# Zero fills of two cache gradients as 16 KB rows, and two more of them ahead of a product stage

## The chip, the cores and the metric

The kernel runs on one core of a Trainium2 chip. A core has TensorE (PE in the profile, with PEld for its weight loads), VectorE (DVE), ScalarE (ACT), GpSimd (POOL) and SyncE (SP), and 16 DMA engines that move data between the device memory and the on-chip memory of 128 partitions. The metric is device time in microseconds (us), lower is better. MB in sizes of tiles is 1,048,576 B.

## The reference, cut to what matters

The reference is one decode step of a transformer block (one token, D = 1024) with its backward pass: the output x2 and the gradients of ten inputs. In short:

```
mod  = silu(c) @ w_mod                       # six sections: sa, ca, ga, sb, cb, gb
h1   = layernorm(x) * (1 + ca) + sa
attn = softmax(q k^T / sqrt(128)) v @ wo     # q = h1 @ wq, 32 heads, 4 cache heads, last 4096 of 65536 positions
x1   = x + ga * attn
h2   = layernorm(x1) * (1 + cb) + sb
x2   = x1 + gb * ((sigmoid(h2 @ w_gate) * (h2 @ w_up)) @ w_down)
outputs: x2, and d(x2 . grad_out) / d(x, k_cache, v_cache, wq, wo, w_gate, w_up, w_down, c, w_mod)
```

Attention reads only the last W = 4096 positions of each cache, so the gradients of k_cache and v_cache (out_2 and out_3, each 4 x 65536 x 128 in bf16) are zero at the first 61,440 positions of each of four heads. These are 8 regions of 15 MB, 120 MB in all, and they have to be written. They are about half of the 246.6 MB that the kernel moves.

## The kernel before, in words

The order of every engine's instructions is written out by hand (`manual_schedule`). Most of the on-chip memory is one tile, `arena`, of 192 KB per partition, whose parts are given out by offset (`ar`); small vectors come from `vt` (L104), each a tile of its own.

The stages, with their place in the profile:

- to about 66 us: small loads, the k cache, wq and v loads (1 MB each, rows of 8 KB per partition), the projections and the softmax;
- 66 to about 160 us, the **N stage** (the long product stage): 128 steps of DVE products and PE matmuls (L632, L637);
- about 160 to 315 us, the **B stage**: chunks of a 4096 x 1024 x 1024 product (`bch`, L682 to L701, matmul at L692), and between them the loads and products for ga, cb, sb and gb, sections of w_mod (`b_sec`, `wm_sec` at L338; `mod_tiles` at L344), transposes and folds (`fold_half`, L871);
- about 315 to 464 us, the **feed-forward stage**: seven blocks. A block loads up and gate weights on POOL's queue (`load_ug`, L865), down weights on SP's queue (`load_wd`, L852), reduces them on DVE (`wd_ttr`, L210), overwrites each tile with its gradient and stores it (`store_ug` on POOL, L869; `store_wd` on SP, L855);
- after it, the attention's backward pass and the remaining stores.

The **zero fills** run through all of it. `zeros` (L111) is a tile of 2,048 one-byte zeros per partition. A fill (L169) is one DMA that POOL issues: 128 partitions of 2,048 bytes, cast from one byte to four, become 128 rows of 8,192 B in the region, 1 MB. Each region is cut into 15 such columns of its 120 KB rows, 120 fills in all. Six of them are narrow (L160 to L167, at the places of NARROW, L38): they leave out eight rows, which one early DMA writes (`zero_rest`, L357), and send a small DMA of their own to move on which DMA engine serves a transfer. That leaves 114 full fills.

`zero(n, after)` (L153) issues the next n fills; with `after` the first instruction of each waits for that instruction ("pace"). The tables say how many go where: Z_Q after the q products, Z_SM (4) after the softmax sums (L523), Z_N (31 over the 128 steps) behind the N stage's matmul six before (L640), Z_B behind the B stage's matmul three before (L694), Z_FOLD at its end, Z_FFN in the feed-forward stage, Z_END after it.

POOL issues all fills, most loads and most stores, in program order, on one DMA queue (queue 0). Its completions use eight semaphores in turn, so each transfer that POOL issues waits for the landing of the one eight before it. SP's transfers go to a queue of their own (queue 1); the 16 DMA engines serve both.

Of the kernel before, what the change touches and what calls it, by code (L numbers as in the profile page):

```python
# [10 lines left out]
P = 128  # L11
FP32 = mybir.dt.float32
BF16 = mybir.dt.bfloat16
# [27 lines left out]
def spread(total, n):  # L41
    return [(i + 1) * total // n - i * total // n for i in range(n)]
# [8 lines left out]
Z_KC = [0] * 8  # L51
Z_SM = 4
Z_N = spread(31, 128)
Z_B = [n + (i in (31, 38)) for i, n in enumerate(spread(29, 43))] + [1, 1, 1, 1, 0] + [1, 1, 0, 1, 1, 0, 1, 1] + [1, 0, 1, 0, 1, 0, 0, 0]
# [4 lines left out]
def kernel(  # L59
# [42 lines left out]

    def vt(shape, name, dt=FP32):  # L104
        return pool.tile(shape, dt, name=name)

    ctx.enter_context(tc.manual_schedule())

    ZW = 4096  # L110
    zeros = vt([P, ZW // 2], "zeros", FP8)  # L111
    rows24 = vt([24, P], "rows24", BF16)
    for k, src in enumerate((A_x[0], grad_out[0], c)):
# [5 lines left out]
    make_identity(nc, ident_f)  # L119
    ones_f = vt([P, P], "ones_f")  # L120
    nc.vector.memset(ones_f, 1.0)

    zregions = []
    for og in (out_2, out_3):
        for g in range(G):
            region = og[0, g, 0:SKW, :].rearrange("r d -> (r d)").rearrange("(p x) -> p x", p=P)
            for i in range(region.shape[1] // ZW):
                zregions.append(region[:, i * ZW:(i + 1) * ZW])

    narrow = zregions[0:len(NARROW)]
    wide = zregions[len(NARROW):]
    zleft = []
    while narrow or wide:
        if narrow and (len(zleft) in NARROW or not wide):
            zleft.append((narrow.pop(0), True))
        else:
            zleft.append((wide.pop(0), False))
    nlen = len(NARROW)
    ncount = list(range(1, nlen + 1))  # L140
    NS = SKIP + 1
# [10 lines left out]

    def zero(n, after=None):  # L153
        for _ in range(n):
            if len(zleft) <= keep[0]:
                return
            region, narrow_ = zleft.pop(0)
            first = None
            if narrow_:
                nc.gpsimd.inc_swdge_sem([], [], mode="reset_dge_cursor")  # L160
                n = nlen - ncount.pop()
                first = nc.gpsimd.dma_start(
                    out=rest[0:NS, 0:nlen * 128].rearrange("p (t x) -> p t x", t=2)[:, :, n * 64:(n + 1) * 64],
                    in_=zeros[0:NS, 0:64].rearrange("p (t x) -> p t x", t=1).broadcast_to([NS, 2, 64]))
                ins = nc.gpsimd.dma_start(
                    out=region[8:P, :].bitcast(FP32).rearrange("(t p) x -> p t x", t=2),
                    in_=zeros[0:60, :].rearrange("p (t x) -> p t x", t=1).broadcast_to([60, 2, ZW // 2]))  # L167
            else:
                ins = nc.gpsimd.dma_start(out=region.bitcast(FP32), in_=zeros[:, :])  # L169
            if after is not None:  # L170
                dep(first or ins, after)

# [79 lines left out]
    def total_bcast(part, ncol, name, scale):  # L253
        ps = new_acc("tot_" + name)
        nc.tensor.matmul(ps[:, 0:ncol], lhsT=ones_f[:, :], rhs=part[:, 0:ncol], start=True, stop=True)
        tot = vt([P, ncol], name)
        ts(tot, ps[:, 0:ncol], float(scale), ALU.mult)
        return tot

    def layernorm_col(x_col, name, gap=lambda: None):  # L260
# [7 lines left out]
        sq = vt([P, KD], name + "_sq")  # L268
# [12 lines left out]

    def layernorm_bwd_col(dln, ln, rstd, name):
        part = vt([P, 2], name + "_parts")
        nc.vector.reduce_sum(out=part[:, 0:1], in_=dln, axis=AX.X)
        tmp = vt([P, KD], name + "_tmp")
# [336 lines left out]
    def recent(mm, lag):  # L622
        last_mm.append(mm)
        return last_mm[-lag] if len(last_mm) >= lag else last_mm[0]

    for g in range(G):
        nbank = bank_pair("n_ps", g)
        for t_ in range(KT):
# [7 lines left out]
            for k in range(2):  # L636
                mm = nc.tensor.matmul(nbank[k][:, :], lhsT=k_nat[:, g, t_ * DH:(t_ + 1) * DH],  # L637
                                      rhs=vp[:, t_ % 2, 4 * k:4 * k + 4, :].rearrange("p h d -> p (h d)"),
                                      start=(t_ == 0), stop=False)
            zero(Z_N[s], recent(mm, 6))  # L640
            if t_ == 20:
# [40 lines left out]
    def bch(n=1):  # L682
        for _ in range(n):
# [238 lines left out]
    bch(1)  # L922
    assert not bq
    fold_half(7, 1)
    zero(Z_FOLD[0])
    park(4, ppq, "pq")
# [88 lines left out]
    side(2)  # L1015
    zero(Z_FOLD[2])
    load_wd(1, 0)
    load_wd(1, 1)
    for q in range(NB):
        z = Z_FFN[q]  # L1020
        more = q + 1 < NB
        for j in range(KD):
# [12 lines left out]
            if j == 3:  # L1035
                store_ug(q, 0, 4)
                zero(z[0])
        store_ug(q, 4, 4)
        zero(z[1])
        if more:  # L1040
# [12 lines left out]
            wd_outer(q + 1, 1)  # L1053
            zero(z[2])
            side()
            if q + 2 < NB:
                load_ug(q + 2, 4, 4)
            zero(z[3])
            if q + 2 < NB:
                load_wd(q + 2, 0)  # L1060
                load_wd(q + 2, 1)
        else:
            zero(z[2] + z[3])
    assert not jobs
# [201 lines left out]
    dwq_tile(3)  # L1266
    x2 = vt([P, KD], "x2")
# [4 lines left out]
    dcsum = vt([P, KD], "dcsum")  # L1272
# [3 lines left out]
    t1 = vt([P, KD], "dc_t1")  # L1276
# [4 lines left out]
    dct = vt([P, KD], "dct")  # L1281
    addv(dct, dcs01[:, :, 0], dcsum)
    addv(dct, dct, dcs)
    dcv = vt([P, KD], "dcv")
    mulv(dcv, t1, dct)
# [17 lines left out]
    zero(len(zleft))  # L1303
    assert not zleft and not narrow and not jobs and not bq

# [28 lines left out]
```

## Time and profile before

| what | value |
|---|---|
| time, median of 3 runs (lowest, highest) | 599.83 us (599.76, 601.25) |
| profiled execution: its time, its span | 597.99 us, 596.2 us |
| busy share of the span: PE, PEld, DVE, ACT, POOL | 69%, 47%, 57%, 44%, 27% |
| DMA packets, MB (10^6 B), mean rate | 45026, 246.63, 414 GB/s |
| fills at L169: transfers, size, median us from issue to landing | 114, 1024 KB, 15.3 |
| issue of one fill on POOL, median | 534 ns |

The profile is of one execution. The span runs from the first instruction of the program to the last; the time has some 1.8 us around it. "DMA share" is the time that packets took divided by that of 16 engines; it can pass 1 because the next packet of an engine can begin while one is in progress. A packet is one contiguous row of a transfer, or some short rows together up to 4 KB; for each of its packets the trace records queue, start, duration and size.

### The profile page before, as it was taken

Reading aid. Unit: us, or ns where it says so; the run is one execution under the profiler, and the core shown is the slowest. Engines: PE = TensorE matmul, PEld = TensorE weight load, DVE = VectorE, ACT = ScalarE, POOL = GpSimd, SP = SyncE. Lnnn points to the kernel's source line nnn. Section 1 sums busy time; section 2 is a strip of 40 time slices with the busy share of each in tenths; the row PEclk is TensorE's granted clock in tenths of the full one; section 3 lists DMA queues with packets and bytes.
Section 4 is the critical chain, followed back from the end, with each engine's and each line's share of the span. In section 5 each row is a group of like instructions: output and inputs, shape, how many; then the busy total and the mean of one; then the engine's idle time right before and its main releaser. Section 6 shows DMA issues by size and latency. Waiting matters only on the chain. (4 is left out here: it accounts for less than half of the span.)

```text
span 596.2 us, 11062 instructions
## 1 busy us (share of the span) xinstructions
PE 412.4 (69%) x4612; PEld 278.2 (47%) x4612; DVE 337.7 (57%) x641; ACT 264.6 (44%) x408; POOL 160.6 (27%) x253
## 2 busy tenths in 40 slices
PE   3997688999999989989984444444445184697220
PEld 3996333334344545546654433434334163586220
DVE  3654498999511010070119495797786985698260
ACT  2489514567211014212234572754745733786110
POOL 3113123222223113222221342423423163233100
PEclk9999699999999999999995555555555586755555
DMA  8999999999999999999999999999999999999997
GB/s 349 419 418 421 411 428 411 427 424 425 428 419 423 423 429 423 420 425 423 423 396 411 420 414 408 391 404 415 408 403 416 420 422 414 421 421 423 425 426 319
DMA packets 45026, 246.63 MB, mean 414 GB/s; under 512 B 5085, under 2 KB 5085, under 8 KB 24544
## 3 DMA queue, kind: packets, MB, share of 16 engines
q0 software_dynamic: 37536, 217.60, 95.1%
q1 hardware_dynamic: 7392, 28.32, 12.4%
q8 instruction: 36, 0.59, 0.4%
q14 instruction: 14, 0.11, 0.1%
q10 hardware_dynamic: 48, 0.01, 0.0%
HBM read 60.30 MB, written 185.60 MB: 412 GB/s over the span
## 5 line engine op out<-in xcount | busy, mean ns | idle before, releaser
L692 PE MATMUL b_ps<-arena 128*128 128x512 bf16 x512 | 116.2, 379 | 0.0
L169 POOL DMA_DIRECT2D out_dram<-zeros x114 | 62.8, 553 | 172.0 <-PE n_ps L637 45.5
L837 PE MATMUL tp_side<-ident_bf,arena 128*128 128x128 bf16 x432 | 51.7, 299 | 54.7 <-ACT arena L838 45.9
L193 DVE TENSOR_TENSOR arena<-arena 128x2048 bf16<-128x2048 bf16 x64 | 76.5, 1223 | 2.3 <-PE n_ps L637 0.3
L692 PEld LDWEIGHTS <-arena 128*128 128x128 bf16 x512 | 48.7, 98 | 55.9 <-issue 2.9
L837 PEld LDWEIGHTS <-arena 128*128 128x128 bf16 x432 | 44.2, 140 | 62.3 <-issue 62.0
L838 ACT COPY arena<-tp_side 128x1024 bf16<-128x1024 bf16 x54 | 54.0, 1013 | 41.8 <-PE tp_side L837 40.9
L637 PE MATMUL n_ps<-arena 128*128 128x512 bf16 x256 | 65.8, 378 | 6.2 <-DVE arena L193 4.6
L210 DVE CUSTOM_DVE_ANT_0 arena<-arena,scr 128x1024 bf16<-128x1024 bf16 x56 | 66.2, 1221 | 3.5 <-ACT scr L993 3.5
L210 DVE CUSTOM_DVE_ANT_0 junk<-arena,b1k 128x1024 bf16<-128x1024 bf16 x28 | 34.3, 1224 | 32.6 <-DMA arena<-in_B_w_down_dram 32.0
L637 PEld LDWEIGHTS <-arena 128*128 128x128 bf16 x256 | 24.6, 97 | 41.6 <-issue 16.2
L241 ACT ACTIVATE arena<-scr,h 128x1024 bf16<-128x1024 bf16 x35 | 39.3, 1148 | 0.0
L202 DVE CAST arena<-b_ps 128x512 bf16<-128x512 f32 x6 | 4.2, 692 | 61.6 <-PE b_ps L692 61.6
L1159 PE MATMUL ps_kv<-junk,arena 8*128 8x128 bf16 x256 | 27.1, 304 | 14.1 <-DVE arena L206 12.8
L1163 ACT ACTIVATE arena<-ps_kv 128x512 bf16<-128x512 f32 x48 | 26.2, 686 | 24.2 <-PE ps_kv L1159 23.7
L601 ACT CAST arena<-t_ps 128x512 bf16<-128x512 f32 x56 | 30.1, 589 | 12.1 <-PE t_ps L599 12.1
L869 POOL DMA_DIRECT2D out_dram<-arena x28 | 21.3, 766 | 51.5 <-ACT arena L241 44.8
L1159 PEld LDWEIGHTS <-arena 8*128 8x128 bf16 x256 | 25.2, 140 | 15.9 <-issue 15.8
L993 ACT COPY scr<-tp_dug 128x1024 bf16<-128x1024 bf16 x7 | 7.1, 1012 | 41.4 <-issue 41.4
L456 ACT COPY arena<-tp_wq 128x1024 bf16<-128x1024 bf16 x23 | 21.8, 1034 | 8.1 <-PE tp_wq L454 8.1
L865 POOL DMA_DIRECT2D arena<-in_B_w_up_dram x14 | 10.5, 753 | 48.3 <-DMA out_dram<-arena 26.2
L206 DVE TENSOR_SCALAR arena<-arena,cs_col 128x4096 bf16<-128x4096 bf16 (+1 forms) x16 | 16.0, 1017 | 10.5 <-DMA out_dram<-arena 10.5
(302 smaller groups left out, 646.9 us busy)
## 6 DMA issues: line engine op xcount, KB each, us to landing
out_dram<-zeros POOLq DMA_DIRECT2D x114, 1024.0 KB, 15.3
out_dram<-arena POOLq DMA_DIRECT2D x27, 1024.0 KB, 17.0
out_dram<-arena POOLq DMA_DIRECT2D x30, 512.0 KB, 11.3
out_dram<-arena SPq DMA_DIRECT2D x20, 512.0 KB, 10.7
arena<-in_A_wq_dram POOLq DMA_DIRECT2D x8, 1024.0 KB, 20.7
arena<-in_A_wo_dram POOLq DMA_DIRECT2D x8, 1024.0 KB, 12.0
arena<-in_w_mod_dram POOLq DMA_DIRECT2D x7, 1024.0 KB, 18.1
arena<-in_B_w_down_dram SPq DMA_DIRECT2D x14, 512.0 KB, 10.0
```

Source lines behind the costliest of these rows:

```text
L169: ins = nc.gpsimd.dma_start(out=region.bitcast(FP32), in_=zeros[:, :])
L193: return nc.vector.tensor_tensor(out=out, in0=a, in1=b, op=op)
L210: return nc.vector.tensor_tensor_reduce(out=out, in0=w, in1=b, scale=1.0, scalar=0.0, op0=ALU.mult, op1=ALU.add, accum_out=acc)
L241: return nc.scalar.activation(out=out, in_=b, func=ACT.Copy, scale=col)
L456: nc.scalar.copy(out=blk, in_=tp[:, :])
L601: nc.scalar.copy(out=o, in_=ps)
L637: mm = nc.tensor.matmul(nbank[k][:, :], lhsT=k_nat[:, g, t_ * DH:(t_ + 1) * DH], rhs=vp[:, t_ % 2, 4 * k:4 * k + 4, :].rearrange("p h d -> ...
L692: mm = nc.tensor.matmul(bbank[p][k][:, :], lhsT=a4[:, p, h, :], rhs=wo_t[u][:, a, k * 512:(k + 1) * 512], start=(i == 0 and a == 0), stop= ...
L837: nc.tensor.transpose(tp[:, i * P:(i + 1) * P], blk[:, i * P:(i + 1) * P], ident_bf[:, :])
L838: nc.scalar.copy(out=blk if dst is None else dst, in_=tp[:, :])
L1159: nc.tensor.matmul(ps[:, t4 * DH:(t4 + 1) * DH], lhsT=rows[32 * g:32 * g + HG, t_ * P:(t_ + 1) * P], rhs=hd[32 * g:32 * g + HG, :], start= ...
L1163: nc.scalar.activation(out=o, in_=ps[:, :], func=ACT.Copy, scale=float(scale))
```

## The change

The zero tile gets twice the width, 4,096 bytes per partition. Outside the feed-forward stage two neighbouring fills become one DMA (L180 of the new kernel): 128 rows of 16,384 B, 2 MB. The regions are cut into such pairs, with single columns where a region has an odd number; when single columns run out, a pair is split. In the N and B stages `paced` adds up what the tables owe and issues a pair at the first of its two dates. In the feed-forward stage, at the narrow fills and where one is left over, fills stay single (L185 of the new kernel). Z_SM goes from 4 to 6 and Z_N from 31 to 29, so that the sum is the same. To make room for the wider zero tile, vectors of fewer than 8 words share one tile (`tiny`), the matrix of ones shrinks to a column that is read with a broadcast, rows24 moves into a part of the arena that is free at the start, and some late vectors reuse earlier ones.

```diff
-Z_SM = 4
-Z_N = spread(31, 128)
+Z_SM = 6
+Z_N = spread(29, 128)
...
+    TINY = 124
+    tiny_t = pool.tile([P, TINY], FP32, name="tiny")
+    tiny_n = [0]
+
     def vt(shape, name, dt=FP32):
+        words = shape[1] if dt == FP32 else (shape[1] + 1) // 2
+        if dt in (FP32, BF16) and words < 8:
+            k = tiny_n[0]
+            tiny_n[0] += words
+            assert tiny_n[0] <= TINY
+            t = tiny_t[:, k:k + words]
+            return t if dt == FP32 else t.bitcast(BF16)
         return pool.tile(shape, dt, name=name)
...
-    zeros = vt([P, ZW // 2], "zeros", FP8)
-    rows24 = vt([24, P], "rows24", BF16)
+    zeros = vt([P, ZW], "zeros", FP8)
+    rows24 = ar(144, 0.25)[0:24, :]
...
-    ones_f = vt([P, P], "ones_f")
+    ones_f = vt([P, 1], "ones_f")
...
+    narrow = [zregions[0][:, i * ZW:(i + 1) * ZW] for i in range(nlen)]
+    pairs, singles = [], []
+    for k, region in enumerate(zregions):
+        i = nlen if k == 0 else 0
+        n = region.shape[1] // ZW
+        if (n - i) % 2:
+            singles.append(region[:, i * ZW:(i + 1) * ZW])
+            i += 1
+        pairs.extend(region[:, c * ZW:(c + 2) * ZW] for c in range(i, n, 2))
+    total = 2 * len(pairs) + len(singles) + nlen
+    zleft = [k in NARROW for k in range(total)]
...
-    def zero(n, after=None):
-        for _ in range(n):
-            if len(zleft) <= keep[0]:
-                return
-            region, narrow_ = zleft.pop(0)
+    def zero(n, after=None, paired=True):
+        while n > 0 and len(zleft) > keep[0]:
             first = None
-            if narrow_:
+            n -= 1
+            if zleft.pop(0):
+                region = narrow.pop(0)
...
+            elif paired and n > 0 and pairs and len(zleft) > keep[0] and not zleft[0]:
+                n -= 1
+                zleft.pop(0)
+                ins = nc.gpsimd.dma_start(out=pairs.pop(0).bitcast(FP32), in_=zeros[:, :])
             else:
-                ins = nc.gpsimd.dma_start(out=region.bitcast(FP32), in_=zeros[:, :])
+                if not singles:
+                    pr = pairs.pop()
+                    singles.extend((pr[:, 0:ZW], pr[:, ZW:2 * ZW]))
+                ins = nc.gpsimd.dma_start(out=singles.pop(0).bitcast(FP32), in_=zeros[:, 0:ZW // 2])
             if after is not None:
                 dep(first or ins, after)
+
+    owed = [0]
+
+    def paced(n, after):
+        owed[0] += n
+        if owed[0] > 0:
+            k = owed[0] + owed[0] % 2
+            owed[0] -= k
+            zero(k, after)
...
-            zero(Z_N[s], recent(mm, 6))
+            paced(Z_N[s], recent(mm, 6))
...
-            zero(Z_B[nbq - 1 - len(bq)], recent(mm, 3))
+            paced(Z_B[nbq - 1 - len(bq)], recent(mm, 3))
...
-    zero(Z_FOLD[0])
+    ahead = -owed[0]
+    zero(Z_FOLD[0] - ahead)
...
-                zero(z[0])
+                zero(z[0], None, False)
```

The other calls in the feed-forward stage change in the same way as the last one.

More of the change, by code (lines that the diff above doesn't have):

```diff
@@ L125 @@
         for g in range(G):
[L126 to L138, printed above, removed]
-    nlen = len(NARROW)
+            zregions.append(og[0, g, 0:SKW, :].rearrange("r d -> (r d)").rearrange("(p x) -> p x", p=P))
+    nlen = len(NARROW)
+    narrow = [zregions[0][:, i * ZW:(i + 1) * ZW] for i in range(nlen)]
[9 more added lines that the diff above has]
+    zleft = [k in NARROW for k in range(total)]
     ncount = list(range(1, nlen + 1))
@@ L150, in dep @@
                           reason="pace")
-    def zero(n, after=None):
-        for _ in range(n):
-            if len(zleft) <= keep[0]:
-                return
-            region, narrow_ = zleft.pop(0)
+    def zero(n, after=None, paired=True):
+        while n > 0 and len(zleft) > keep[0]:
             first = None
-            if narrow_:
+            n -= 1
+            if zleft.pop(0):
+                region = narrow.pop(0)
                 nc.gpsimd.inc_swdge_sem([], [], mode="reset_dge_cursor")
-                n = nlen - ncount.pop()
+                k = nlen - ncount.pop()
                 first = nc.gpsimd.dma_start(
-                    out=rest[0:NS, 0:nlen * 128].rearrange("p (t x) -> p t x", t=2)[:, :, n * 64:(n + 1) * 64],
+                    out=rest[0:NS, 0:nlen * 128].rearrange("p (t x) -> p t x", t=2)[:, :, k * 64:(k + 1) * 64],
                     in_=zeros[0:NS, 0:64].rearrange("p (t x) -> p t x", t=1).broadcast_to([NS, 2, 64]))
@@ L166, in zero @@
                     out=region[8:P, :].bitcast(FP32).rearrange("(t p) x -> p t x", t=2),
-                    in_=zeros[0:60, :].rearrange("p (t x) -> p t x", t=1).broadcast_to([60, 2, ZW // 2]))
-            else:
-                ins = nc.gpsimd.dma_start(out=region.bitcast(FP32), in_=zeros[:, :])
+                    in_=zeros[0:60, 0:ZW // 2].rearrange("p (t x) -> p t x", t=1).broadcast_to([60, 2, ZW // 2]))
+            elif paired and n > 0 and pairs and len(zleft) > keep[0] and not zleft[0]:
+                n -= 1
+                zleft.pop(0)
+                ins = nc.gpsimd.dma_start(out=pairs.pop(0).bitcast(FP32), in_=zeros[:, :])
+            else:
+                if not singles:
+                    pr = pairs.pop()
+                    singles.extend((pr[:, 0:ZW], pr[:, ZW:2 * ZW]))
+                ins = nc.gpsimd.dma_start(out=singles.pop(0).bitcast(FP32), in_=zeros[:, 0:ZW // 2])
             if after is not None:
                 dep(first or ins, after)
+    owed = [0]
[5 more added lines that the diff above has]
+            zero(k, after)
     rot = [(psum, "mm")]
@@ L254, in total_bcast @@
         ps = new_acc("tot_" + name)
-        nc.tensor.matmul(ps[:, 0:ncol], lhsT=ones_f[:, :], rhs=part[:, 0:ncol], start=True, stop=True)
+        nc.tensor.matmul(ps[:, 0:ncol], lhsT=ones_f[:, 0:1].broadcast_to([P, P]), rhs=part[:, 0:ncol], start=True, stop=True)
         tot = vt([P, ncol], name)
@@ L258, in total_bcast @@
         return tot
+    bwd_tmp = vt([P, KD], "bwd_tmp")
     def layernorm_col(x_col, name, gap=lambda: None):
@@ L267, in layernorm_col @@
         ts(xc, x_col, mean[:, 0:1], ALU.subtract)
-        sq = vt([P, KD], name + "_sq")
+        sq = bwd_tmp
         part2 = vt([P, 1], name + "_p2")
@@ L284, in layernorm_bwd_col @@
         nc.vector.reduce_sum(out=part[:, 0:1], in_=dln, axis=AX.X)
-        tmp = vt([P, KD], name + "_tmp")
+        tmp = bwd_tmp
         ttr(tmp, dln, ln, part[:, 1:2])
@@ L922 @@
     bch(1)
-    assert not bq
+    assert not bq and owed[0] in (0, -1)
+    ahead = -owed[0]
     fold_half(7, 1)
-    zero(Z_FOLD[0])
+    zero(Z_FOLD[0] - ahead)
     park(4, ppq, "pq")
@@ L1015 @@
     side(2)
-    zero(Z_FOLD[2])
+    zero(Z_FOLD[2], None, False)
     load_wd(1, 0)
@@ L1036 @@
                 store_ug(q, 0, 4)
-                zero(z[0])
+                zero(z[0], None, False)
         store_ug(q, 4, 4)
-        zero(z[1])
+        zero(z[1], None, False)
         if more:
@@ L1053 @@
             wd_outer(q + 1, 1)
-            zero(z[2])
+            zero(z[2], None, False)
             side()
@@ L1057 @@
                 load_ug(q + 2, 4, 4)
-            zero(z[3])
+            zero(z[3], None, False)
             if q + 2 < NB:
@@ L1062 @@
         else:
-            zero(z[2] + z[3])
+            zero(z[2] + z[3], None, False)
     assert not jobs
@@ L1266 @@
     dwq_tile(3)
-    x2 = vt([P, KD], "x2")
+    x2 = a3[:, 0:8]
     mulv(x2, gb, ffn)
@@ L1271 @@
     col_to_row_out(dx0, out_1[0], "dx0", late.pop())
-    dcsum = vt([P, KD], "dcsum")
+    dcsum = a3[:, 8:16]
     addv(dcsum, dcs234[:, :, 0], A3[:, :, 2])
@@ L1275 @@
     stt(dcsum, A3[:, :, 1], rm[:, 1:2], dcsum, ALU.mult, ALU.add)
-    t1 = vt([P, KD], "dc_t1")
+    t1 = a3[:, 16:24]
     ts(t1, sig_c, -1.0, ALU.mult, 1.0, ALU.add)
@@ L1280 @@
     mulv(t1, t1, sig_c)
-    dct = vt([P, KD], "dct")
+    dct = a_lo[:, 0:8]
     addv(dct, dcs01[:, :, 0], dcsum)
     addv(dct, dct, dcs)
-    dcv = vt([P, KD], "dcv")
+    dcv = a_lo[:, 8:16]
     mulv(dcv, t1, dct)
@@ L1303 @@
     zero(len(zleft))
-    assert not zleft and not narrow and not jobs and not bq
+    assert not zleft and not narrow and not pairs and not singles and not jobs and not bq
 _INS = ['A_x', 'A_k_cache', 'A_v_cache', 'A_wq', 'A_wo', 'B_x', 'B_w_gate', 'B_w_up', 'B_w_down', 'c', 'w_mod', 'grad_out']
```

## The prediction, made before the changed kernel ran

> **What bounds the kernel now.** I read the page's slices first, then the queues, the stages in windows, the waits, and last two windows of the DMA view in which only one kind of transfer runs.
>
> ```profile
> DMA  8999999999999999999999999999999999999997
> GB/s 349 419 418 421 411 428 411 427 424 425 428 419 423 423 429 423 420 425 423 423 396 411 420 414 408 391 404 415 408 403 416 420 422 414 421 421 423 425 426 319
> ...
> q0 software_dynamic: 37536, 217.60, 95.1%
> q1 hardware_dynamic: 7392, 28.32, 12.4%
> ```
>
> The 16 DMA engines are busy in every slice but the first and last, at 391 to 429 GB/s. 246.6 MB pass through them, and no compute engine comes near (PE 69%, and 50% of its clock in the later half). Counting the trace's packet records, 16 or more packets are in flight nearly always from 2 us to 588 us. So the time is the sum of what the packets cost, plus about 8 us at the ends. Work taken from the DMA engines shortens the kernel, unless a queue then runs dry; delays elsewhere cost only where one runs dry.
>
> ```profile
> core 0: us, PE busy (x) PEld busy (x) DVE busy (x) ACT busy (x) POOL busy (x), PEclk, DMA share, GB/s
> ...
> 66.00:160.00 94.00, 85.32 (x433) 36.61 (x431) 82.24 (x89) 44.89 (x110) 24.80 (x44) 0.96 1.13 422
> 160.00:300.00 140.00, 134.61 (x1107) 73.57 (x1106) 24.44 (x63) 29.25 (x43) 34.29 (x59) 1.00 1.13 423
> ...
> 315.00:464.00 149.00, 67.67 (x1011) 59.72 (x1009) 112.15 (x234) 81.93 (x93) 48.60 (x70) 0.50 1.08 409
> ```
>
> From 66 to 300 us PE is as full as the DMA engines (85.3 of 94 us, 134.6 of 140). That stage's length belongs to PE. What faster fills save there is not seen there: it leaves a shorter queue for the feed-forward stage, from which on only the DMA engines are full. The third row is that stage, at 409 GB/s.
>
> ```profile
> POOL out_dram L169 <- PE n_ps L637: 45.5, 22, 6.3
> POOL out_dram L169 <- DMA out_dram<-zeros: 36.5, 18, 3.9
> ...
> PE g_ps L344 <- DMA arena<-in_w_mod_dram: 0.7, 1, 0.7
> ```
>
> These are waits from 66 to 315 us. POOL waits 18 times until an earlier fill has landed: it has eight completion semaphores, and its ninth transfer waits for its first. The landings show the queue: a fill issued at 86 us lands after 7.6 us, one at 250 us after 20. PE waits for a load once, for 0.7 us.
>
> **What a row costs.** Two windows of the DMA view, the first with fills alone, the second with loads in 8 KB rows:
>
> ```profile
> DMA packets 709, 5.12 MB, mean 427 GB/s; under 512 B 82, under 2 KB 82, under 8 KB 86
> q0 software_dynamic: 709, 5.12, 114.6%
> ```
> ```profile
> DMA packets 1725, 12.56 MB, mean 419 GB/s; under 512 B 197, under 2 KB 197, under 8 KB 197
> ```
>
> A fill's packets overlap (share 114.6%), a load's do not, and the fill is the faster. In the packet records loads and stores have a median of 309 ns at 8,192 B and 159 ns at 4,096 B: 150 ns for 4,096 B, so 300 ns for the bytes of an 8 KB row and 9 ns that do not grow with them. Between 100 and 300 us one fill lands 2.435 us after the one before it (median). An engine writes 8 rows and one 4-byte completion packet in that time: 2,435 - 8 x 300 = 35 ns per fill do not grow with bytes.
>
> **The change part by part.**
>
> 1. *Pairs.* Of the 114 full fills 80 become 40 pairs in the order of POOL's instructions; 34 single ones, all of the feed-forward stage among them, and the six narrow ones stay. A pair is 8 rows of 16,384 B per engine and one completion: 8 x 600 + 35 = 4.835 us against 2 x 2.435 = 4.870. **Saved: 0.035 us x 40 = 1.4 us.** No queue that carries data has a 16 KB packet in this trace, so I bound it. Upper end, the loads' row: 9 ns for each of 8 rows and a completion of 9 ns are 81 ns a pair, 3.2 us. Lower end: nothing, if the rows are cut in two on their way. A loss per row I exclude: the only 16,384 B packets are the instruction queue's 36, with a median of 1,022 ns, and one such packet at 609 ns (by the slope) beside one fill packet (348 ns) is 957 ns, inside their 10% to 90% span of 936 to 1,090. I take 1.4 us, because fills are what becomes longer.
>
> The Trainium skill's "DMA: Bandwidth & Descriptors", section "Where 436 GB/s comes from", sets a ceiling of 435.2 GB/s for the 16 engines, at which an estimate for 80 MB leaves 2.1 us above the fills' rate and halving it gives 1.05 us; that speaks against the upper end. The same page's "SDMA does more than copy" gives 2,048 elements as the most its inline adder takes at once; the fills cast one byte to four and a 16 KB row has 4,096 elements, so if a cast obeyed that, the saving would be nothing. No run here shows it.
>
> 2. *POOL.* 40 issues of 0.53 us go: 21 us on an engine at 27%. They lie beside the transfers and are worth nothing. The eight semaphores now cover up to 16 MB, so POOL waits less for landings; the order of the bytes in its queue is what counts, and that hardly moves.
>
> 3. *Six ahead, and pairs sent at the first of their two dates.* Fills move ahead of loads in POOL's queue. By count, loads of w_o have 16, 18, 24, 32, 40 fills ahead instead of 14, 15, 23, 31, 39; they are used from 156 us on and land from 69 to 174 us, so this is hidden. The second half of the ga load has 53 ahead instead of 52. It lands at 210.96 us and is used here:
>
> ```profile
> L344 PE MATMUL ga_ps<-cs_bf,arena x64: 162/163/166, 211.9 to 213.5; 128*128 128x1 bf16 x64
> ```
>
> One fill later (+2.4) and 23 pairs cheaper (-0.8) it lands at 212.6: **a new wait of 0.7 us** on PE. Behind it stand the rest of the long products, and behind those the start of the feed-forward stage. It costs nothing while the DMA queue holds 15 to 18 us of work there (a fill issued at 315.8 us lands 17.2 us later); without that cover it costs 0.7. The later loads have as many fills ahead as before, or one more with 6 us to spare (242.95 and 245.48 against 252.0).
>
> 4. *The zero tile's memset* doubles, 0.48 to about 0.97 us, at 0.9 us; DVE's next work comes at 6.18 us. *The ones column, the small tiles in one buffer, the reused tiles at the end:* the same instructions stand in the same order on PE and DVE with the same kinds of waits. ScalarE gains one wait, for loads that ended some 50 us before it. All nothing.
>
> Sum: 597.99 us (the profiled execution; its span is 596.2, and 1.8 lies around it) - 1.4 = 596.6. The median of the three runs is 599.83, 1.84 above the profiled one; I carry the saving to the median: **598.4 us**, 0.23% less. About 0.3%, 1.8 us, is what a measurement of this kernel can tell from no change, so my likeliest case lies within it.
>
> **The rivals.**
>
> *A, the forecast:* 598.4 us, chance 0.42. For it: fills are measured, and the DMA engines are never idle. Its own spread, with runs from 599.76 to 601.25 before, is about 0.8 us either way; 0.12 of the 0.42 falls beyond 1.8 us of gain.
>
> *B, a 16 KB row saves what a load's row shows:* 3.2 us, 596.6, chance 0.28. For it: 9 ns are seen at 2, 4 and 8 KB alike (85, 159, 309). Against it: a fill's packets overlap and already hide half of that.
>
> *C, it does not do what it says:* rows are cut, the packets stay at 8 KB, and only issues go. 599.8 us, chance 0.13.
>
> *D, slower:* a packet holds its engine until it is done, and SP's queue takes turns with POOL's. Beside fills a turn of SP is 159 + 304 = 463 ns; beside pairs 159 + 609 = 768. The w_mod loads on SP at 295.5 and 301.8 us have 8 packets per engine each: 8 x 0.305 = 2.4 us later, and on the second PE already waits. The first down-projection stores (319.29 us) run beside the last fills for 3.5 us: 7.5 turns become 4.5, and 3 packets at 318 ns are made up later, 0.95 us. With the 0.7 us of ga that is 4.1 us, and 599.83 + 4.1 = 603.9, chance 0.17. It decides if the feed-forward stage's chain (store, load, two DVE reductions) and not the queue sets its pace. For it: a fill's time to landing falls from 17 us at 316 to 7 to 9 us at 372, and from 372 to 380 us the rate is 366 and 359 GB/s with fewer than 16 packets in flight for a tenth of the time. Against it: even there the DMA share is 1.01 or more, and the low rate goes with loads in 1 KB rows (382 GB/s from 304 to 312 us, with a full queue).
>
> *How the numbers follow:* faster by over 0.3%: B 0.28 + 0.12 of A = 0.40. Within: 0.30 of A + C 0.13 = 0.43. Slower: D 0.17. The range takes in A, C and B down to 0.6 below its centre, and leaves out D's centre and B's tail: 596.0 to 600.8.
>
> **What would show it.** Pairs: packets of 16,384 B on queue 0, 5,120 of them, and some 427 to 430 GB/s becoming 430 to 434 in windows of fills alone. If the spacing of pairs is 4.87 us or the packets are 8 KB, C holds; at 4.79 us, B. Part 2: waits of POOL for landed fills fall from 36.5 us. Part 3: a wait of PE at the ga product of about 0.7 us. D would show as a longer wait of the g_ps product for w_mod, a feed-forward stage that starts after 315 us, and less than 16 packets in flight more often at 370 to 380 us. The forecast is wrong if the feed-forward stage runs the queue dry, so that what was saved before it is lost as idle engines.

## The result, and the profile after

The changed kernel takes 605.01 us (median of 20 runs, 600.81 to 607.84); the kernel before, on the same chip, 600.02 us (20 runs, 598.32 to 601.95). The ratio is 1.0081, 95% interval 1.0066 to 1.0096: slower by 0.8%, where 598.4 us was forecast. A ratio here and below leaves out single runs over 1.5% above the fastest of their kernel (one each of e4, e9 and e13) and is not the quotient of the medians beside it. The runs of the changed kernel are spread over 7 us, those of the kernel before over 3.6. The profiled execution (607.84 us, span 606.1) is the longest of its 20, so what follows shows the loss at its largest.

From the page of the changed kernel, the slices of the DMA engines and the two queues:

```profile
DMA  8999999999999999999999599999999999999997
GB/s 352 418 418 425 413 429 426 431 428 424 430 426 421 431 429 419 435 419 428 408 412 360 197 404 418 381 397 411 404 405 407 416 420 416 421 419 426 425 423 304
...
q0 software_dynamic: 31776, 217.59, 91.2%
q1 hardware_dynamic: 7392, 28.32, 12.4%
```

The same bytes go out in 5,760 packets less. The loss is seen at once: two slices at 360 and 197 GB/s, where nothing of the kind stood before. The same in windows, now cut at the hole:

```profile
core 0: us, PE busy (x) PEld busy (x) DVE busy (x) ACT busy (x) POOL busy (x), PEclk, DMA share, GB/s
66.00:160.00 94.00, 84.42 (x435) 36.92 (x443) 82.80 (x90) 45.85 (x112) 16.12 (x27) 0.99 1.07 427
160.00:300.00 140.00, 130.75 (x1029) 70.69 (x1045) 24.12 (x62) 26.99 (x40) 23.55 (x39) 0.96 1.07 425
...
328.00:346.00 18.00, 8.10 (x88) 6.91 (x89) 17.01 (x36) 11.41 (x14) 1.94 (x3) 0.50 0.58 206
```

The last of these windows in the kernel before:

```profile
328.00:346.00 18.00, 8.61 (x144) 7.66 (x143) 10.03 (x23) 8.34 (x11) 5.81 (x8) 0.50 1.14 420
```

From 66 to 300 us the queue moves 427 and 425 GB/s instead of 422 and 423: by the packet records 126.33 MB have gone out by 300 us instead of 125.57, a lead of 0.76 MB or 1.8 us. Then 18 us at 206 GB/s; at 380 us the lead has become a lag of 2.94 MB, 7 us. In sum the 16 engines stand idle for 8.5 us between 250 and 480 us, before for 0.3 (from the packets in flight, those of 4 bytes left out; one us means all 16 idle for one us). The second row has one more novelty: PE's clock was 1.00 there before, and is 0.96.

What PE waits for, 66 to 330 us, and the ga product:

```profile
PE g_ps L371 <- DMA arena<-in_w_mod_dram: 6.2, 2, 4.4
...
PE b_ps L719 <- DMA arena<-in_A_wo_dram: 0.9, 1, 0.9
```
```profile
L371 PE MATMUL ga_ps<-tiny,arena x64: 163/163/178, 211.0 to 213.5; 128*128 128x1 bf16 x64
...
  DMA arena<-in_w_mod_dram: 0.8, 1
```

(L371 and L719 are L344 and L692 of the kernel before.) The 0.8 us at ga has the place and the size that were forecast, and the load lands at 212.62 us, forecast 212.6; why the size is luck is said further down. The 0.9 us at 176 us was not: the last load of w_o, with 40 fills ahead of it instead of 39, lands at 175.97. And g_ps, the last product ahead of the feed-forward stage, waits 6.2 us for w_mod instead of 0.7.

The instructions of SP's queue, with the time of the first of each pair, in the kernel before and in the changed one:

```profile
295.49 6.62 SPq L338 DMA_DIRECT2D arena<-in_w_mod_dram  x2
319.29 1.14 SPq L855 DMA_DIRECT2D out_dram<-arena  x2
327.70 4.54 SPq L852 DMA_DIRECT2D arena<-in_B_w_down_dram  x2
```
```profile
301.97 6.62 SPq L365 DMA_DIRECT2D arena<-in_w_mod_dram  x2
332.11 1.62 SPq L882 DMA_DIRECT2D out_dram<-arena  x2
335.43 1.53 SPq L879 DMA_DIRECT2D arena<-in_B_w_down_dram  x2
```

PE's products give the last two w_mod loads free 6.5 us later. The second of them then takes 13.1 us to land (321.41) instead of 7.5 (309.27), the feed-forward stage's first matmul comes at 326.0 instead of 313.2, its first store at 332.1 instead of 319.3, and meanwhile POOL's queue, which has only its own 15 us in hand, runs dry. So three links are to be explained: how waits of 0.8 and 0.9 us become 6.5 us, why 6.5 us become 12.8, and why the queue does not cover that.

In the trace of PE's granted clock there are three stretches of half clock inside the products, 3.4 us each, at 213.9, 224.1 and 258.2 us. The kernel before has none between 73 and 312 us. Each costs up to 1.7 us of PE's time, three 5.1. In this execution PE had come 2.0 us early to the products (b_ps at 154.3 instead of 156.4, the full clock having come sooner); less these, with the two waits, that is 4.8 us, and the md_ps product (sb's) at 288.3 is 4.6 late. A wait of 2.2 us inside its second half, up to 296.6, which the profile puts down to nothing ("issue"), makes it the 6.5. Seven of the traced executions have a wait there (after, e3, e4, e6, e12, e13, e16; 0.5 to 2.4 us), and in each it ends 1.3 to 1.5 us after a 16,384 B packet of the instruction queue q8 has ended (295.10 us here). In the kernel before that packet ends at 282.77, long before PE is there. So PE may be waiting for its own instructions; no run tests it.

### The profile page after: what moved, and what is told of

The parts are those of the page before. It is cut to its first block, busy times and chain, and to the rows that moved or that the text cites. A ratio compares the mean times of both kernels' runs of the same rounds, so it can differ in the third digit from the quotient of the medians.

```text
span 606.1 us, 10967 instructions
## 1 busy us (share of the span) xinstructions
PE 414.2 (68%) x4587; PEld 279.2 (46%) x4612; DVE 338.7 (56%) x641; ACT 264.8 (44%) x408; POOL 138.0 (23%) x213
## 5 line engine op out<-in xcount | busy, mean ns | idle before, releaser
L719 PE MATMUL b_ps<-arena 128*128 128x512 bf16 x494 | 117.8, 389 | 2.1 <-DMA arena<-in_A_wo_dram 0.9
L719 PEld LDWEIGHTS <-arena 128*128 128x128 bf16 x512 | 50.0, 100 | 59.8 <-issue 9.4
L864 PEld LDWEIGHTS <-arena 128*128 128x128 bf16 x432 | 44.8, 142 | 62.3 <-issue 62.1
L180 POOL DMA_DIRECT2D out_dram<-zeros x40 | 21.7, 543 | 134.3 <-PE b_ps L719 52.8
L664 PEld LDWEIGHTS <-arena 128*128 128x128 bf16 x256 | 24.6, 97 | 41.6 <-issue 16.2
L1187 PE MATMUL ps_kv<-junk,arena 8*128 8x128 bf16 x256 | 26.5, 299 | 16.2 <-DVE arena L231 14.3
L185 POOL DMA_DIRECT2D out_dram<-zeros x34 | 19.3, 570 | 32.1 <-PE q_ps L499 14.3
## 6 DMA issues: line engine op xcount, KB each, us to landing
arena<-in_w_mod_dram POOLq DMA_DIRECT2D x7, 1024.0 KB, 16.2
```

The costliest lines, as they stand in the source:

```text
L180: ins = nc.gpsimd.dma_start(out=pairs.pop(0).bitcast(FP32), in_=zeros[:, :])
L864: nc.tensor.transpose(tp[:, i * P:(i + 1) * P], blk[:, i * P:(i + 1) * P], ident_bf[:, :])
L1187: nc.tensor.matmul(ps[:, t4 * DH:(t4 + 1) * DH], lhsT=rows[32 * g:32 * g + HG, t_ * P:(t_ + 1) * P], rhs=hd[32 * g:32 * g + HG, :], start= ...
```

## The experiments

Theory 1, after the traces: the w_mod loads come to stand behind pairs, and that is the loss. Theory 2: the loss begins earlier, with loads that have one fill more ahead of them. Rival: the 16 KB rows themselves, as rival D had it. All ratios are to runs of the kernel before on the same chip (medians 599.35 to 599.60 us).

**One part alone, one part undone**

*e2: six ahead alone, in the kernel before.*

```diff
-Z_SM = 4
-Z_N = spread(31, 128)
+Z_SM = 6
+Z_N = spread(29, 128)
```

> The kernel before with six single fills ahead of the N stage instead of four (29 instead of 31 in it). Theory 1 (the last two w_mod loads on SP's queue stand still behind fills at the end of the B stage): nothing changes there, within 1 us of before. Theory 2 (loads that get one more fill ahead make PE late): the ga loads keep 49 and 52 fills ahead, so within 1 us of before too; w_o loads get 15, 17, 24 ahead and have time. If sending fills ahead were the cause by itself: 3 to 5 us slower than before.

598.88 us, ratio 0.9975 (0.9952 to 0.9998); feed-forward stage at 312.9 us, no half-clock stretch, idle engines 0.6 us. Six ahead is not the loss. It is no proven gain either: e8 below, in effect the kernel before once more, has 0.9982.

*e3: the pairs in rows of 8 KB.*

```diff
-out=pairs.pop(0).bitcast(FP32), in_=zeros[:, :]
+out=pairs.pop(0).bitcast(FP32).rearrange("p (t x) -> p t x", t=2),
+in_=zeros[:, 0:ZW // 2].rearrange("p (t x) -> p t x", t=1).broadcast_to([P, 2, ZW // 2])
```

> The changed kernel with the same 40 pairs at the same places, but each written as two rows of 8 KB per partition. If the 16 KB row is the cause (a packet that holds its engine twice as long): back to within 1 us of before, about 600. Theories 1 and 2 (place and order of the fills, not their rows): still 3 to 6 us slower than before, with a feed-forward stage that starts some 8 to 13 us late. The saving of the rows, if there is any, would show as the difference to the changed kernel: up to 1 us.

607.12 us, ratio 1.0097 (1.0062 to 1.0132), with half-clock stretches at 222.7 and 256.8 us, a wait of 6.9 us at g_ps and 7.2 us of idle engines. The long row is innocent, and with it rival D's mechanism.

*e5: pairs sent at the second of their two dates (and four ahead).*

```diff
-Z_SM = 6
-Z_N = spread(29, 128)
+Z_SM = 4
+Z_N = spread(31, 128)
...
-        if owed[0] > 0:
-            k = owed[0] + owed[0] % 2
+        if owed[0] > 1:
+            k = owed[0] - owed[0] % 2
```

> The changed kernel with four fills ahead again and each pair sent at the second of its two dates, so that no load has more fills ahead of it than before. Theory 2: PE no longer waits for the w_o and ga loads, the SP loads of w_mod are issued at about 295 and 301 us as before, and the time is 598 to 600.5. Theory 1 with another cause of the lateness, or the 16 KB rows as cause: still 3 us or more slower than before.

600.68 us, ratio 1.0014 (0.9990 to 1.0039): w_o's loads have 14, 14, 22, 30, 38 fills ahead and ga's second half 51. No PE wait for either, no half-clock stretch, feed-forward stage at 313.6. Theory 2 holds.

*e4: two pairs taken from between block 0's loads and block 1's and put behind the latter.*

```diff
-... + [1, 0, 1, 0, 1, 0, 0, 0]
-Z_FOLD = (1, 1, 2)
+... + [0, 0, 0, 0, 0, 0, 0, 0]
+Z_FOLD = (0, 5, 2)
```

> The changed kernel with the two pairs that stand ahead of the second block's up and gate loads moved behind these loads. Theory 1: the last two w_mod loads on SP run beside loads in 4 KB packets and land 5 to 8 us after their issue instead of 13 to 15; the feed-forward stage starts by 321 us, the DMA queue is not empty before it, and the time is 598.5 to 601. Theory 2 alone (PE is late by 6 us and everything follows): the w_mod loads may land sooner, but the feed-forward stage still starts 6 us late, 602 to 604.

605.76 us, ratio 1.0077 (1.0041 to 1.0114), expected 598.5 to 601: a miss. The w_mod loads are no longer awaited, and the feed-forward stage begins at 318.1. But the pairs were missing where they had stood: block 1's loads are issued only from 311.2 us on, and from 304 to 320 us the engines move 213 GB/s. And the first store on SP's queue, issued at 324.1 us, now met the moved pairs and took 16.2 us. It cleared the place in question and spoiled two others, so it decides nothing between the theories.

**The first link: one fill**

*e6: the kernel before, one fill earlier.*

```diff
+Z_B[15] += 1
+Z_B[16] -= 1
```

> The kernel before with nothing changed but the date of one 8 KB-row fill: it goes ahead of the second half of the ga load instead of behind it (53 fills ahead instead of 52; every other load keeps its count). It asks what the first link of the chain costs by itself. Theory (a short PE wait is multiplied by the clock): the load lands at 213.4, PE waits 1 to 1.5 us for it, at least one half-clock stretch of 3.4 us follows between 213 and 300 (there is none in the kernel before), so PE is 2.5 to 5 us late at 298, the two w_mod loads on SP's queue go out at 298 or later instead of 295.5, and the time is 601 to 605. Rival, as the prediction had it (a wait costs itself and the full queue hides it): no half-clock stretch, PE 1 to 1.5 us late, time 599 to 600.

607.86 us, ratio 1.0097 (1.0063 to 1.0131). No pairs, no six ahead: one 8 KB-row fill ahead of one load. PE waits 0.8 us at ga, half-clock stretches follow at 214.9, 225.2, 259.3 (6.8 us long) and 300.3, and the feed-forward stage begins at 328.2. Expected were 601 to 605 us: one fill ahead of one load costs more than that, 1.0%, and the whole change 0.8%.

*e13: the reverse, in the changed kernel: one date moved behind the second ga load.*

```diff
+Z_B[14] -= 1
+Z_B[16] += 1
```

> The changed kernel with one date moved behind the second ga load, so that 51 fills stand ahead of it instead of 53; the pairs, the first of the two dates, six ahead and every other load's count stay (the two w_o loads still have 40 instead of 39). It is the smallest undoing. Theory (ga's wait is the first link): the load lands at about 208, PE waits for nothing there, no half-clock stretch from it, feed-forward stage at 313 to 316, time 598.5 to 601. If the late w_o loads (a wait of 0.9 us at 176) suffice to start the same chain: 603 to 607 with half-clock stretches after 176 and no ga wait.

604.28 us, ratio 1.0059 (1.0024 to 1.0094), runs from 600.32 to 609.51. In the profiled execution there is no wait at ga, one of 0.3 us for w_o, and there are stretches at 221.1, 255.2 (6.8) and 296.2. Of the two outcomes written down for it this is the second. So a fill ahead of ga is enough (e6), but ga's wait is not needed. That the 0.3 us brought the stretches is not shown either; the table below says why.

**How a wait becomes three stretches**

The starts of all half-clock stretches of an execution lie a whole number of 3.413 us apart (213.88, 224.12 and 258.25 us in the changed kernel: 3 and 10 times): the clock is judged in windows of a fixed grid. And PE has one long wait of its own in this stage, 2.14 us for the layernorm at about 219 us, in every kernel. Where it lies in that grid sorts the executions (us; "lost" is what PE waited for loads between 100 and 215 us):

| execution | lost | the 2.14 us wait begins, after a window's edge | half clock after it |
|---|---|---|---|
| before, e9 (e8 is a repeat of before) | 0 | 2.67, 2.73 (2.64) | no |
| e11, e14, e15, e2, e5 | 0 | 2.93, 3.05, 3.12, 3.14, 3.15 | no |
| changed, e4 | 1.7, 1.5 | 0.05, 3.41 | yes |
| e3, e10, e12 | 0.5, 0.2, 0.9 | 0.14, 0.17, 0.30 | yes |
| e13, e6 | 0.3, 0.8 | 0.32, 0.62 | yes |
| e16, e17 (below) | 0 | 0.38; 2.86 | yes; no |

Begun at 2.6 to 3.2, the wait lies across an edge and spoils two windows a little; begun at 0 to 0.6 (or just at the edge), it lies in one and takes most of it. Without the time lost it would have begun at 3.0 in e3 and at 2.8 in e12, places that no half clock follows in the other executions. In e13 and e10, whose full clock had come at 67.5 and 67.2 us, it would have begun at 0.0 and 3.3, so there the waits of 0.3 and 0.2 us may not have mattered.

In the changed kernel, e4 and e6 one more stretch comes first, at 213.9, 213.8 and 214.9 us, and there the wait at ga has a part of its own. The window ahead of it holds ga's whole product, of 128x1 matmuls, and the wait; in the changed kernel:

```profile
210.47:213.88 3.41, 2.57 (x69) 2.06 (x68) 0.19 (x2) 0.00 (x0) 0.00 (x0) 1.00 1.06 426
```

In e13 the same product lies in one window without a wait (PE busy for 3.33 us), and no half clock follows at its end. So in the changed kernel both waits and this stretch, 1.7 us more, bring PE to the place in the grid that the table gives.

To see whether the grid is the cause, PE is moved in e16 and e17 without any wait:

*e16 and e17: four, or sixteen, useless matmuls ahead of the ga product in the kernel before.*

```diff
+    idle_ps = new_ps("idle_ps")
+    for i in range(4):        # 16 in e17
+        nc.tensor.matmul(idle_ps[:, :], lhsT=ident_bf[:, :], rhs=v_nat[:, 0, 0:512], ...)
```

> The kernel before with four useless matmuls (128x512, 0.21 us each) put ahead of the ga matmuls: PE comes 0.85 us later to the layernorm at 219 us; no load is late, no fill is moved, and no engine waits more. Grid theory: the 2.1 us wait now begins 0 to 0.3 us into a window of the 3.413 us grid instead of 2.7 us into one and fills it, a half-clock stretch follows at about 223, others near 257, PE is 4 us or more late at 290 and the time is 603 to 608. Rival (a wait for a DMA is what brings the stretches): no stretch, PE 0.85 us late, time within 1 us of the kernel before.

> The same with sixteen such matmuls, 3.41 us, one whole window of the grid. Grid theory: PE comes back to the place in the grid that it has in the kernel before, no half-clock stretch between 200 and 300, PE 3.4 us late at 290, the last w_mod load goes out at 305.2 instead of 301.8, and the time is 599 to 602.5 (the late load may cost something by itself), under that of four matmuls. Rival (more lateness, more loss): over that of four matmuls.

Four take 604.0 us, ratio 1.0066 (1.0044 to 1.0089); sixteen 602.89 us, ratio 1.0053 (1.0033 to 1.0074). The windows of the grid around the layernorm, of the kernel before:

```profile
216.45:219.86 3.41, 2.65 (x14) 1.36 (x12) 0.42 (x3) 0.20 (x1) 0.53 (x1) 1.00 1.16 432
219.86:223.28 3.42, 2.04 (x16) 1.22 (x17) 1.19 (x9) 1.53 (x3) 0.00 (x0) 1.00 1.16 431
```

of e16:

```profile
219.44:222.86 3.42, 1.28 (x15) 0.93 (x14) 1.61 (x11) 0.61 (x2) 0.00 (x0) 1.00 1.15 426
222.86:226.27 3.41, 3.41 (x10) 1.17 (x9) 0.00 (x0) 2.15 (x4) 0.37 (x1) 0.50 1.15 430
```

and of e17:

```profile
219.44:222.86 3.42, 2.86 (x15) 1.45 (x13) 0.31 (x2) 0.14 (x1) 0.53 (x1) 1.00 1.15 426
222.86:226.27 3.41, 1.82 (x15) 1.12 (x16) 1.30 (x9) 1.38 (x4) 0.00 (x0) 1.00 1.17 435
```

The second number is PE's busy time. In e16 it is 1.28 us of one window, and the next runs at 0.50; before it is 2.65 and 2.04, in e17 2.86 and 1.82, and the clock stays at 1.00. Four times the added work, and no stretch between 73 and 300 us in the profiled execution: PE is late by about its 3.4 us (fold product at 269.4 instead of 266.2), where e16 with 0.85 us of work is 5.3 late (271.5). That the place in the grid decides is shown by these traces. The times do not tell the two kernels apart: their intervals overlap, e16's profiled execution (607.23 us) is the longest of its 12, and e17 is over the 599 to 602.5 expected. Its last w_mod load goes out at 305.0 us and makes g_ps wait 4.7 us.

It may also be why the kernel before is steadier: its full clock comes at an edge of the grid, and from there PE runs without a wait for a load, so that ga begins 138.8 to 139.3 us later in all seven executions without a wait that got their full clock at 71.7 to 73.3 us. From its 2.67 to the 3.15 of e5 a margin of 0.5 us is seen to be safe, no more. Its runs of 603 to 606.5 us, which the chips of the experiments have too, were not traced.

**The second link: a load on SP's queue behind fills**

*e8: the two w_mod loads written two chunks later in the kernel before.*

> The kernel before with its two w_mod loads on SP's queue issued one place later each in PE's order, so at about 302 and 308 us, as in the changed kernel, instead of 295.5 and 301.8; no pairs, no other fill moved, no PE wait ahead of them. It asks whether the late loads alone cost the time. Theory (SP's queue stands still while fills are at the front of POOL's): the second load is not down before the fills that follow block 0's loads have gone, so it takes 10 us or more, the feed-forward stage begins at 320 or later instead of 313.2, the DMA engines are idle for 4 us or more between 320 and 350, and the time is 602 to 606. Rival (the queues share; what the changed kernel loses it loses by PE's lateness in the products): the load takes 7 to 8 us as before, the stage begins by 317.5, idle under 2 us, time under 601.

599.12 us, ratio 0.9982 (0.9962 to 1.0002), loads issued at 295.4 and 301.7 as before: SP's queue holds them until the matmuls that read their buffer are done, wherever the line stands. The edit moved nothing, and the run is a second measurement of the kernel before.

*e11: the same with a dependency.*

```diff
+    def late_wm(j):
+        dep(nc.sync.dma_start(out=g_t[j], in_=wm_view[:, j, 5 * D:6 * D]), last_mm[-1])
-    wm_sec(5, 4, 1, 58, nc.sync)
-    wm_sec(5, 5, 1, 60, nc.sync)
+    late_wm(4)      # where (5, 5) stood
+    late_wm(5)      # two chunks later
```

> The kernel before with its two w_mod loads on SP's queue made to wait for later products of PE (an added dependency on the last matmul of the chunk two places on), so that they go out at about 301.8 and 308.1 us as in the changed kernel, with PE itself on time and no half-clock stretch ahead. It asks whether late loads alone cost the time. Theory (a load on SP's queue that is not down when block 0's loads end, at 313, stands behind the fills until about 323): the second load takes 12 us or more, the feed-forward stage begins at 322 or later, the DMA engines are idle for 3 us or more between 320 and 350, and the time is 602 to 606. Rival (the queues share, and the loss belongs to PE's lateness): the load lands within 8 us, the stage begins by 317.5, time under 601.

606.38 us, ratio 1.0121 (1.0091 to 1.0152), with PE on time and no half-clock stretch. The loads go out at 301.0 and 305.8 us, and the second lands at 319.1. PE's waits and the windows of e11:

```profile
PE g_ps L344 <- DMA arena<-in_w_mod_dram: 11.1, 2, 10.2
```
```profile
320.00:350.00 30.00, 15.91 (x252) 14.06 (x250) 21.09 (x44) 16.29 (x20) 6.16 (x9) 0.50 0.91 332
```

So late w_mod loads alone bring the loss. Why the second takes 13 us is seen in the DMA view, 302 to 308 us before:

```profile
q0 software_dynamic: 425, 1.58, 71.1%
q1 hardware_dynamic: 331, 0.67, 31.2%
```

and 309 to 315 us after, with SP's two loads outstanding all the time:

```profile
q0 software_dynamic: 191, 2.55, 105.7%
q1 hardware_dynamic: 34, 0.06, 21.5%
```

Beside block 0's loads, whose rows are 1,024 B (four of them to a 4,096 B packet), SP's queue q1 sends 331 packets in 6 us. Beside pairs it sends 34. In e11, beside fills of 8 KB, 312 to 317 us:

```profile
q0 software_dynamic: 279, 2.01, 106.8%
q1 hardware_dynamic: 68, 0.11, 24.1%
```

By then only 56 rows of SP's two loads were left there, and they took 4.3 us. In the kernel before the fills behind block 0's loads come to the front from 308 us on and are alone on queue 0 from 313; the last w_mod load, landed at 309.27, was just ahead of them, and 6.5 us late it isn't.

*e9 and e12: the other way round, one w_mod load made early.* It goes to b1k (issued at 266.8 us in e9), is copied to its home by ACT, and the last load takes the first one's place.

```diff
...
+    g_t[4] = b1k
+    nc.sync.dma_start(out=b1k, in_=wm_view[:, 4, 5 * D:6 * D])
     load_wd(0, 0)
...
-    wm_sec(5, 4, 1, 58, nc.sync)
+    wm_sec(5, 5, 1, 58, nc.sync)
...
-    wm_sec(5, 5, 1, 60, nc.sync)
...
+    nc.scalar.copy(out=ar(60, 2), in_=b1k)
...
```

> The changed kernel with the first of the two w_mod loads put into a buffer that is free 50 us earlier (it is copied to its home by one ACT copy afterwards), so that only one load is gated by the last products, at the place in PE's order where the first one was (about 301.9 us instead of 308.3 for the last one). Pairs, six ahead, late loads of w_o and ga, half-clock stretches: all unchanged. Theory (the loss falls where w_mod's loads come to stand behind pairs): the last load goes out at the date that it has in the kernel before, lands by 312, the feed-forward stage begins at 318 to 320, idle engines under 3 us, time 600 to 602, 3 us or more under the changed kernel. Rival (6 us of lateness of PE is lost at the end whatever the loads do): 604 to 606, with the idle time at another place.

> The kernel with one fill ahead of the second ga load (607.9) and the early w_mod load added: the half-clock stretches stay, the last w_mod load goes out one place sooner in PE's order. Theory (the loss is the load that comes to stand behind fills, PE's lateness of 5 to 8 us costs little by itself): last w_mod load issued at about 306 instead of 312.4, feed-forward stage at 318 to 322 instead of 328.2, idle engines under 3 us instead of 7.7, time 600 to 603. Rival (lateness is lost whatever the loads do): 606 to 609.

e12 (e6 with the early load): 600.36 us, ratio 1.0025 (1.0001 to 1.0048), where e6 has 607.86. Three of e6's four half-clock stretches are there (223.8, 257.9 for 6.8 us, 298.9; none at 214), PE is 6.2 us late at the fold product (e6: 7.8), and the last load, issued at 304.3, lands at 313.2; feed-forward stage at 321.4, idle engines 3.0 us. By the medians PE's lateness by itself costs about 1 us and the load behind fills the other 7. But the profiled execution of e12, in which the lateness is seen, took 602.85 us, and that of e6 609.20: between these two the split is nearer 3 and 6.

e9 (the changed kernel with it): 601.15 us, ratio 0.9994 (0.9964 to 1.0025), runs from 597.86 to 606.87. Its profiled execution had no stretch at all, so it tells nothing of that link; what its six runs over 602 us lose is not known. It tells something of the first. The last w_o load and the second ga load land at 176.03 and 212.67 us, as in the changed kernel, and PE waits for neither, because its full clock came at 73.3 us and not at 67.1, and it is 2.3 us later at b_ps. So whether the same fills make PE wait depends on the execution. The runs of the changed kernel lie in two groups (nine at 600.8 to 603.6 us, nine at 606.6 to 607.8), which would fit; only one of them was traced.

**Versions that might beat both**

> The kernel before with six fills ahead instead of four and the same early w_mod load (no pairs): a version that may beat both. Theory: the last w_mod load goes out at 294.7 instead of 301.0, the feed-forward stage begins 2 to 4 us before 312.9, and the time is 597 to 599 (0.2 to 0.5% under the kernel before); were the stage's start not what sets the end, 598.9 as with six ahead alone.

> Pairs sent at the second of their dates, four ahead (600.7), with the early w_mod load: a version that may beat both kernels and shows what the pairs are worth when no load is late. Theory: feed-forward stage begins at 308 to 312, no idle engines, time 597 to 599, which is the 1.4 us of the pairs and up to 1 us more under the kernel before. If the pairs save nothing: 599 to 600, as the kernel before.

> The changed kernel (pairs, six ahead) with pairs sent at the second of their dates, so that no load has more fills ahead of it than in the kernel before plus one, and the early w_mod load: all three parts of what was learned. If pairs save what the fills' landings say (0.03 to 0.035 us for each of 39 pairs): no half-clock stretch, 597 to 598.5, 0.8 to 1.5 us under the same without pairs (598.9). If their saving is used up elsewhere: 598.5 to 600.

| kernel | us | ratio to before | range of runs |
|---|---|---|---|
| e2: six ahead | 598.88 | 0.9975 (0.9952 to 0.9998) | 598.0 to 602.2 |
| e10: six ahead, early load | 598.90 | 0.9974 (0.9956 to 0.9991) | 598.0 to 599.7 |
| e15: pairs at the second date, six ahead, early load | 599.13 | 0.9981 (0.9957 to 1.0005) | 598.1 to 600.8 |
| e14: the same, four ahead | 600.95 | 1.0021 (1.0008 to 1.0034) | 598.8 to 602.7 |

None of them is clearly under the kernel before: e8, which changes nothing, has 0.9982. e2, e10 and e15 cannot be told apart. e10 has the narrowest runs, and its profiled execution gives a likely reason: half-clock stretches at 220.8 and 254.9 us made PE 3 us late at the fold product, and the span is still 597.0. Pairs show no gain in e15 and e14. e14's median, 2 us over its own profiled execution (598.79, no stretch, 0.6 us idle), stays unexplained; its other executions were not traced.

## Why the prediction was wrong

*Step 1, pairs: right in size, worth nothing in the end.* 5,120 packets of 16,384 B; pairs land 4.845 us apart (median), twice the 2.436 of the kernel before is 4.872: 0.027 us each, where 0.035 was forecast, 1.1 us for 40 instead of 1.4. Rivals B (3.2 us) and C (rows cut) are out. The lead of 0.76 MB at 300 us is real too. That it reaches the end was an assumption. e9's profiled execution, undisturbed, leads the kernel before by 0.79 MB at 300 us and by 0.14 MB (0.3 us) at 560. Where the rest goes between was not settled.

*Step 2, POOL: right.* Its waits for landed fills fall from 36.5 to 12.0 us, and no loss was traced to it.

*Step 3: this failed.* The landing of ga's load was forecast to a tenth of a us, but that the wait came out at 0.8 is luck. The forecast set the landing against the first matmul of ga, at 211.9 us; the half that lands last is used by the 33rd of the 64, which in the kernel before comes at 212.71, after 212.62. The wait arose because PE, its full clock having come 6 us sooner, was at ga 0.95 us earlier; in e9, with the same landing, there is none. The same holds for the 40th fill ahead of the last w_o load, called hidden: by the timing of the kernel before PE would have come to that load at about 177 us, and it landed at 175.97; in the profiled execution PE came at 175.1 and lost 0.9 us.

The step that decides is the price of a wait. That price, nothing "while the DMA queue holds 15 to 18 us of work there", was worked out as if a wait costs its length and nothing but the length of the queue stood between PE and the end. The runs show in its place: a delay of 0.5 to 0.9 us (waits in e3 and e12, useless matmuls in e16) moves PE's own 2.14 us wait into one window of the clock's grid, and with the stretches of half clock that follow PE loses 4 to 6 us more (e16, e6); and that delay takes the last w_mod load past the end of block 0's loads, behind the fills, which adds 6 to 7 us to the time (e11; e6 against e12). Against that the 15 us of queue did not suffice: the engines stood idle for 8.5 us. PE's lateness also holds back block 1's loads (311.6 us instead of 309.5), which are part of what should fill the queue; what share of the loss that is was not tested.

*Step 4: right*; no loss was traced to it, and e15, which has all of it, takes 599.13 us.

*Rival D* had the right side and the right place (the g_ps wait, a stage that starts after 315 us, the end decided by idle engines) with the wrong mechanism. It priced SP's turns beside longer packets at 2.4 us. With 8 KB rows the loss is the same (e3, e6, e11), and beside fills SP's queue gets far less than a turn for each row (34 packets against 191, 68 against 279). It took the dates of the w_mod loads, 295.5 and 301.8 us, as fixed; in the changed kernel they are 6.5 us later. The last sentence of the forecast, that it is wrong if the feed-forward stage runs the queue dry, is what happened.

The Trainium skill bears on two of the links. "TensorE: Matmul & The Clock Gate", section "What's actually happening", gives a free-running window of 3,413 ns and half clock after an idle one; the grid of the stretches agrees. Its advice in "Why this matters for your kernels", no gaps over about 3 us, is too mild here: a gap of 2.14 us in one window was enough (e16). "DMA: Bandwidth & Descriptors", section "Queues, rings and completion order", has each DMA engine go round-robin between queues, a packet of some 9 to 17 descriptors at a turn. What the trace records are then descriptors, nine for each engine in a pair (8 rows and a completion); as many of q1 for each pair would be an estimate of 16 x 9 in 4.85 us, 178 in 6 us. The runs show 34.

## What to carry to other kernels

A wait is priced by where it puts the instructions behind it, not by its length alone: look what those free (a buffer, a load on another queue), and what stands in the way of it then. Before moving a transfer ahead of a load that lands within 1 us of its use, take the load out of the way first; a load that decides the start of the next stage should be given a buffer that is free early. Before a landing is set against a use, look which matmul of the product reads that part of the load, and by how much PE's own timing differs from one execution to the next. And when runs of a kernel spread over 1% with the same work, look whether a pause of one engine falls differently into the clock's windows.

## What was not expected of the hardware

- PE's clock is judged on a fixed grid of 3.413 us. Windows in which PE was busy for 1.28 us (e16) brought half clock in the next; 1.82 (e17) and 2.04 us (before) did not, nor did 1.53 us (e5, 218.62 to 222.03 us). Busy time alone does not settle it: in the changed kernel a window with 2.57 us of PE, most of it 128x1 matmuls, ahead of 213.9 us was followed by half clock as well.
- Where the full clock begins in the load stage sets where PE lies in the grid 140 us later. Among the traced executions of these kernels it came between 66.7 and 75.0 us; in the changed kernel and e9, which are the same program up to there, at 67.1 and 73.3.
- Beside fills that cast 1 byte to 4 (2 MB or 1 MB each), q1 got 34 packets of 2,048 B and less in 6 us beside pairs and 68 in 5 us beside 1 MB fills; beside loads in 4,096 B packets it got 331, of up to 4,096 B, in 6 us. With the queue empty a store of SP landed 3.3 us after its issue, beside fills 8 to 16 us.
